# A first cluster assignment of two heads on split partitions, another order of the first loads, and other planner costs, in a kernel of clustered attention and two MLPs

## The chip, the cores and the metric

The kernel runs on one core of a Trainium2 chip. The metric is the device time of one execution in microseconds. Engines: TensorE (PE in the rows, its weight loads PEld), VectorE (DVE), ScalarE (ACT), GpSimd (POOL) and SyncE (SP), which here issues every DMA, one after the other on one queue.

## The reference, cut to what matters

Attention has 2 batches, 8 heads, 768 positions and 64 columns a head. Every query and key is put into one of 16 clusters of its head, and a query sees only the keys of its own cluster. The output (1536 tokens by 512) goes through a squared-ReLU MLP (512 to 2048 to 512) and a gated MLP (512 to 1536 to 512).

```python
q_assign = np.argmax(np.einsum('bhsd,hcd->bhsc', q_n, c_n), axis=-1)
k_assign = np.argmax(np.einsum('bhsd,hcd->bhsc', k_n, c_n), axis=-1)
mask = q_assign[:, :, :, None] == k_assign[:, :, None, :]
scores = np.where(mask, scale * np.matmul(q, k.transpose(0, 1, 3, 2)), -1000000000.0)
attn = np.exp(scores - np.max(scores, axis=-1, keepdims=True))
attn = attn / (np.sum(attn, axis=-1, keepdims=True) + 1e-09)
x = np.matmul(attn, v)              # then laid out as tokens x 512
h = np.maximum(x @ w_in, 0.0)
x = h * h @ w_out
out = (1.0 / (1.0 + np.exp(-(x @ w_gate))) * (x @ w_val)) @ w_out2
```

## The kernel before

**Tiles.** A score tile is 128 queries by 768 keys of one head: 96 tiles, numbered 0 to 95, six a head (n // 6 is the head, batch 0 first). For each, TensorE makes `s` (`t_qk`, L821), VectorE the negative row maximum `nm` (`t_max`), ScalarE the exponential (`t_exp`), ScalarE an upper f16 part `hl` (`t_hi`) and VectorE the lower f16 part into the same `hl` (`t_lo`). A DMA transpose turns two tiles into `pt` (`t_turn`, L878), TensorE multiplies them by the values into `po` (`t_pv`), and VectorE scales `po` into `xp` (`t_x`). The pairs of tiles in the list `by_pe` take another way: TensorE transposes the f32 tile (`tb`, L906), and nothing is split.

**The mask** is part of the score product. A head has query rows `T` and key rows `M`: 64 rows of numbers, split into a rounded part and a remainder by subtraction (`qlo` L776, `klo` L782), and 16 rows that say which cluster a column belongs to. Copies on ScalarE, VectorE or GpSimd build these tiles for head 1 and later heads (the helper `copy` has L317, L319 and L321 for the three engines); DMAs put the cluster rows in (`dup`, L752, L753). Head 0 has its own tile `TM`.

**The assignment** of four heads is one group. TensorE writes 16 dots a column into `as` (`assign_dots`, L419): 128 partitions are 2 (queries or keys) x 2 pairs of heads x 32, and the 768 columns lie in two halves of 384. VectorE then does seven steps over 128x768 (`assign_steps`, L440: transpose `d`, maximum `mx`, `eq`, `w`, maximum `m`, `eq`, transpose back `ot`), after which two writes at 16x768 fill `TM` (L559 and the copy behind it) and `assign_end` (L498) makes `oh` for the other heads. Group 0 is written out by hand before the planner starts and needs the loads of two pairs of heads.

**Magnitudes of the values.** ScalarE takes |v| of the six tiles of a batch (`v_abs`, L510, tile `jk`); VectorE reduces them to `a` (L515), TensorE and VectorE make a scale `sc` of it, by which the values are split in two f16 parts `vh`, `vl`.

**Weights** come as 64-bit words in staging tiles (two of them during attention, tiles `wi0r`, `wo0r`), are turned to f32 (L1172 to L1201), and split in two parts (`wi0h`, `wi0l`). The first MLP runs on chunks of 512 tokens. Chunk 0 (batch 0's first tokens) is worked into the attention of batch 1: `g` is a block of the first product, `y` of the second. `xq` are the transposes of the attention's output. From the fourth `y` group of chunk 0 on (`y0_3`) only MLP work is left, and TensorE does it in a fixed order.

**The order** of all that follows group 0 is made when the program is built. `Planner` keeps a list of tasks, each with a cost in ns for every engine that could do it (`{"v": 869, "p": 1660}`) and a priority (tile number minus an offset from `PLAN`); it starts on each engine the ready task with the lowest priority and adds `SETTLE` until a result can be read. A task may only move to another engine if it would end sooner there by its price (cost plus offsets). Tasks of VectorE and GpSimd that use a shared port are not planned side by side (`port`). `Planner({...})` (L253) holds the planned time at which each engine is free after the part by hand. On the chip every engine then runs its list in order and waits for semaphores.

## Time and profile before

| | us |
|---|---|
| median of 3 runs (830.93 to 834.58) | 832.7 |
| profiled execution | 831.97 |
| its span, first to last instruction | 830.2 |
| TensorE busy | 766.0 (92%) |
| VectorE busy | 547.9 (66%) |
| ScalarE busy | 447.8 (54%) |
| GpSimd busy | 266.4 (32%) |

The profiled execution is 1.8 us longer than its span. Busy shares are means over two stages that differ: attention with chunk 0 of the MLP worked in, up to about 345 us, and the rest of the MLPs. The mean granted clock of TensorE is 0.968 of 2.4 GHz over the span.

### The profile page before, as it was taken

What the parts mean: (1) busy time and instruction counts of PE and PEld (TensorE: products, weight loads), DVE (VectorE), ACT (ScalarE), POOL (GpSimd) and SP (SyncE); (2) the same over time, 40 slices, a digit from 0 to 9 for tenths busy, and PEclk for the clock granted to TensorE, in tenths of its full rate; (3) what the DMA queues carried; (4) which work ended last, traced back from release to release, by engine and by line L of the source; (5) the groups of instructions that cost most, each with busy time, mean ns of one, the idle gap of its engine ahead of it and who ended that gap; (6) DMA issues with size and microseconds to landing.
All of it is one profiled execution on the core that took longest, in us unless ns stands there. A gap on an engine that the chain in (4) does not pass through costs nothing.

```text
span 830.2 us, 12473 instructions
## 1 busy us (share of the span) xinstructions
PE 766.0 (92%) x4721; PEld 633.7 (76%) x4721; DVE 547.9 (66%) x865; ACT 447.8 (54%) x800; POOL 266.4 (32%) x322
## 2 busy tenths in 40 slices
PE   8778687789888979799999999999999999999998
PEld 4468576668776868688888888888888888888886
DVE  5689888989999998868376776924333427933300
ACT  2989767778887675758564563422212225612300
POOL 3955646486555323334041322111111113100000
PEclk9889789999999989999999999999999999999999
DMA  6599997966889788732232322411211222100101
GB/s 201 137 191 211 181 191 158 214 130 137 165 207 212 180 194 185 268 102 95 83 127 76 102 80 98 135 68 54 98 51 51 76 78 102 51 24 27 39 26 38
DMA packets 143420, 100.56 MB, mean 121 GB/s; under 512 B 124128, under 2 KB 124128, under 8 KB 143360
## 3 DMA queue, kind: packets, MB, share of 16 engines
q1 hardware_dynamic: 143360, 99.76, 47.4%
q8 instruction: 37, 0.61, 0.3%
q14 instruction: 23, 0.19, 0.1%
HBM read 62.10 MB, written 3.15 MB: 79 GB/s over the span
## 4 chain that ended last, share of the span: by engine, by line
PE 68%; DVE 11%; DMA 8%; ACT 6%; issue 4%; POOL 1%; SPq 1%; DVEq 0%; POOLq 0%; ACTq 0%
PE y L310 14%; PE o L310 12%; PE pv L310 12%; PE pg L310 12%; PE g L310 11%; DMA pt<-hl 5%; DVE nm L839 3%; PE po L310 3%; PE s L310 3%; DMA wo0r<-in_moe_w_out_dram 2%; DVE hl L869 2%; ACT s L854 2%; ACT hl L317 2%; DMA raw<-in_k_dram 1%; DVE M L319 1%
## 5 line engine op out<-in xcount | busy, mean ns | idle before, releaser
L310 PE MATMUL s<-M,T 128*128 128x384 f32 x360 | 88.5, 375 | 28.2 <-DVE hl L869 14.2
L839 DVE TENSOR_REDUCE nm<-s 128x1 f32<-128x768 f32 x96 | 90.3, 950 | 10.6 <-PE s L310 9.9
L310 PEld LDWEIGHTS s<-M,T 128*128 128x128 f32 x360 | 65.2, 204 | 38.8 <-issue 14.1
L1442 DVE SCALAR_TENSOR_TENSOR gv<-th,pv 128x512 f32<-128x512 f32 x36 | 24.6, 687 | 98.2 <-PE pv L310 98.2
L1435 ACT ACTIVATE th<-pg 128x512 f32<-128x512 f32 x36 | 21.5, 598 | 123.9 <-PE pg L310 120.1
L854 ACT ACTIVATE s<-s,nm 128x768 f32<-128x768 f32 x78 | 68.1, 873 | 24.1 <-DVE nm L839 23.7
L869 DVE TENSOR_TENSOR hl<-s,hl 128x768 f16<-128x768 f32 x78 | 73.7, 948 | 4.0 <-ACT hl L317 3.6
L310 PEld LDWEIGHTS <-pt 128*128 128x128 f16 x1404 | 49.4, 104 | 24.0 <-DMA pt<-hl 13.8
L310 PE MATMUL po<-vh,pt 128*128 128x64 f16 x936 | 53.9, 202 | 13.8 <-DMA pt<-hl 9.1
L317 ACT ACTIVATE hl<-s 128x768 f16<-128x768 f32 x78 | 63.3, 811 | 1.9
L310 PE MATMUL po<-vl,pt 128*128 128x64 f16 x468 | 51.0, 202 | 0.0
L1471 ACT ACTIVATE ot<-o 128x512 f32<-128x512 f32 x12 | 7.2, 599 | 81.0 <-PE o L310 81.0
L1369 ACT ACTIVATE r<-g 128x512 f32<-128x512 f32 x48 | 28.7, 598 | 26.5 <-PE g L310 26.4
L1180 POOL TENSOR_SCALAR wgm<-wgm 128x512 f32<-128x512 f32 x12 | 7.7, 643 | 104.5 <-ACT wgm L1172 92.9
L1411 DVE TENSOR_TENSOR yf<-yf,y 128x512 f32<-128x512 f32 x36 | 24.7, 685 | 17.9 <-PE y L310 17.5
L776 POOL TENSOR_TENSOR T<-raw,T 64x768 fp32r<-64x768 f32 x15 | 29.3, 1954 | 4.1 <-ACT T L317 3.1
L782 POOL TENSOR_TENSOR M<-raw,M 64x768 fp32r<-64x768 f32 x15 | 28.3, 1887 | 1.4 <-DVE M L319 0.5
L1375 ACT ACTIVATE g<-r 128x512 f32<-128x512 f32 x47 | 28.3, 601 | 0.9
L1298 DVE TENSOR_TENSOR gs_0l<-gv,gs_0h 128x512 fp32r<-128x512 f32 x3 | 2.1, 690 | 39.3 <-ACT gs_0h L317 39.3
L1180 POOL TENSOR_SCALAR wi1m<-wi1m 128x512 f32<-128x512 f32 x16 | 10.4, 652 | 52.6 <-ACT wi1m L1172 45.6
L310 PEld LDWEIGHTS po<-vr,ptf 128*128 128x128 f32 x216 | 25.6, 192 | 0.2 <-DVE xp L961 0.2
L310 PE MATMUL po<-vr,ptf 128*128 128x64 f32 x216 | 25.6, 272 | 0.0
(583 smaller groups left out, 2359.5 us busy)
## 6 DMA issues: line engine op xcount, KB each, us to landing
wi0r<-in_moe_w_in_dram SPq DMA_DIRECT2D x16, 512.0 KB, 4.3
wo0r<-in_moe_w_out_dram SPq DMA_DIRECT2D x16, 512.0 KB, 4.0
wi1r<-in_moe_w_in_dram SPq DMA_DIRECT2D x16, 512.0 KB, 3.4
wo1r<-in_moe_w_out_dram SPq DMA_DIRECT2D x16, 512.0 KB, 3.3
wgr<-in_moe_w_gate_dram SPq DMA_DIRECT2D x12, 512.0 KB, 3.2
wvr<-in_moe_w_val_dram SPq DMA_DIRECT2D x12, 512.0 KB, 4.2
w2r<-in_moe_w_out_dram SPq DMA_DIRECT2D x12, 512.0 KB, 4.0
raw<-in_q_dram SPq DMA_DIRECT2D x8, 384.0 KB, 4.0
```

The source lines that it names most:

```text
L310: nc.tensor.matmul(o, lhsT=l, rhs=r, start=a, stop=z)
L317: nc.scalar.activation(out=out, in_=in_, func=AF.Copy, scale=scale)
L776: eng(e).tensor_tensor(out=T1[j][q], in0=raw[k][r], in1=T1[j][r].bitcast(F32), op=ALU.subtract)
L782: eng(e).tensor_tensor(out=M2[j][r], in0=raw[k][r], in1=M1[j][r].bitcast(F32), op=ALU.subtract)
L839: nc.vector.tensor_reduce(out=NM[n], in_=sc_ps[n][:, :, :HS], axis=AX.XY, op=ALU.max, negate=True)
L854: nc.scalar.activation(out=y, in_=x, func=AF.Exp, bias=NM[n], accum_out=SM[n // NQ][:, i : i + 1],)
L869: nc.vector.tensor_tensor(out=halves(hl[:, n % 2, 1]), in0=x[:, :, :HS], in1=halves(hl[:, n % 2, 0]), op=ALU.subtract,)
L1369: nc.scalar.activation(out=r, in_=banks["g1", c, f], func=AF.Relu)
L1375: nc.scalar.activation(out=p, in_=r, func=AF.Square)
L1411: nc.vector.tensor_tensor(out=yf[c, dm], in0=yf[c, dm], in1=p, op=ALU.add)
L1435: nc.scalar.activation(out=t, in_=p, func=AF.Tanh, scale=0.5)
L1442: nc.vector.scalar_tensor_tensor(out=o, in0=t, scalar=1.0, in1=p, op0=ALU.add, op1=ALU.mult)
```

## The change

The first group is cut in two. `pair_dots` makes the dots of two heads only, and puts the two halves of the 768 columns on different partitions, so that the seven steps run over 128x384. Heads 2 and 3 become a group of their own (numbered -1 in the code; its tiles are called `d4`, `ot4`, `oh4` in the built program), which the planner places. `oh` of these two groups is half as wide; its rows go to a head by four DMAs instead of two. The by-hand `oh` of the first group moves to GpSimd.

The first loads are issued in another order: queries and keys of the first pair of heads, the keys of head 0 for `TM`, the six value tiles, and then the second and third pair. Before, the second pair stood ahead of the values. A table load for the exponential is asked for early by a one-column activation (`warm`). The products that keep TensorE busy during the first assignment are 7 instead of 11 and read the keys instead of the queries.

The planner gets other costs (loads, DMA transposes, subtractions on GpSimd), other offsets in `PLAN` (nearly all of some 70; one line of them is shown), other times of the first tasks, a list `by_pe` of ten pairs instead of nine, and a reserve of slabs for the first chunk (`xn`). `NS`, `e_bufs` and `third` come to the same numbers as before, and `by_pool` is empty.

```diff
-SETTLE = {"t": 200, "v": 120, "a": 130, "p": 130, "q": 2500}
+SETTLE = {"t": 200, "v": 120, "a": 130, "p": 130, "q": 2100}
...
+    "asg_p": -800, "assign": 15, "assign_step": 2.0, "base": 70, "build": 4, "build2": 5.9,
...
-    "by_pe": (1, 7, 8, 16, 19, 24, 26, 30, 33,),
+    "by_pe": (1, 7, 10, 13, 16, 19, 24, 26, 30, 33,),
...
-    NS = 34
+    NS = 37 - (3 * PLAN["e_bufs"] + 1) // 2
...
-    WARM = (10, 11)
+    WARM = (10, 7)
...
-    plan = Planner({"t": 16300, "v": 16700, "a": 5600, "p": 6500, "q": 14100})
+    plan = Planner({"t": 13900, "v": 14000, "a": 5600, "p": 13600, "q": 17500})
...
+    units.update({"xn": 2 * KD})
...
-    for p in range(2):
-        for s in range(2):
-            load_raw(s, 0, p)
+    for s in range(2):
+        load_raw(s, 0, 0)
     nc.sync.dma_start(out=MN[0:64], in_=kT[0, 0, 0:64])
     for t in range(NQ):
         load_v(0, t)
-    for s in range(2):
-        load_raw(s, 0, 2)
+    for p in range(1, 3):
+        for s in range(2):
+            load_raw(s, 0, p)
...
+    warm = at.tile([P, 1], F32, name="warm")
+    nc.scalar.activation(out=warm, in_=rt, func=AF.Exp, scale=0.0)
...
+    def pair_dots(gp):
+        a = s_tile(f"as_{-gp}")
+        for s in range(2):
+            for hf in range(2):
+                r0 = s * 64 + hf * 32
+                mm(
+                    a[r0 : r0 + 32, 0, :HS], CB[:, -gp].rearrange("p j c -> p (j c)"),
+                    raw[s, 0, -gp][:, hf * HS : (hf + 1) * HS], True, True,
+                )
+        assign_tiles(gp, a)
...
-        OH[gp] = at.tile([P, S], F32, tag="oh", name=f"oh{gp}")
+        n = S if gp > 0 else HS
+        OH[gp] = at.tile([P, S], F32, tag="oh", name=f"oh{gp % (NG + 1)}")
         eng(e).tensor_scalar(
-            out=OH[gp], in0=AS[gp]["ot"], scalar1=aux_a, scalar2=aux_b, op0=ALU.mult, op1=ALU.add
+            out=OH[gp][:, :n], in0=AS[gp]["ot"][:, :n], scalar1=aux_a, scalar2=aux_b,
+            op0=ALU.mult, op1=ALU.add,
...
-    assign_dots(0)
+    pair_dots(0)
     nc.scalar.activation(out=TN[0:64], in_=raw[0, 0, 0][0:64], func=AF.Copy, scale=0.125)
-    keep_busy(raw[0, 0, 0][:, :HS], WARM[1])
+    keep_busy(raw[1, 0, 0][:, :HS], WARM[1])
     drop(busy)
-    for f, _ in assign_steps(0, 1):
+    for f, _ in assign_steps(0, 2):
         f(0)
     drop(AS[0]["a"])
     ot = AS[0]["ot"]
-    nc.vector.tensor_scalar(
-        out=MN[64 : 64 + C], in0=ot[64 : 64 + C], scalar1=BIG, scalar2=-BIG,
-        op0=ALU.mult, op1=ALU.add,
-    )
-    copy("v", TN[64 : 64 + C], ot[0:C])
-    assign_end(0)
+    for hf in range(2):
+        c = slice(hf * HS, (hf + 1) * HS)
+        nc.vector.tensor_scalar(
+            out=MN[64 : 64 + C, c], in0=ot[64 + 32 * hf : 64 + 32 * hf + C, :HS],
+            scalar1=BIG, scalar2=-BIG, op0=ALU.mult, op1=ALU.add,
+        )
+        copy("v", TN[64 : 64 + C, c], ot[32 * hf : 32 * hf + C, :HS])
+    assign_end(0, "p")
...
-                    lambda e, s=s, b=b, p=p: load_raw(s, b, p), {"q": 1092},
+                    lambda e, s=s, b=b, p=p: load_raw(s, b, p), {"q": 1600},
...
-    ohhold = {0: hold("oh", 1, 3)}
-    for gp in range(1, NG):
-        b, gr = divmod(gp, H // 4)
+    ohhold = {0: hold("oh", 1, 1)}
+    for gp in [-1] + list(range(1, NG)):
+        b, gr = divmod(max(gp, 0), H // 4)
         keys = [(s, b, 2 * gr + pl) for s in range(2) for pl in range(2)]
         pr = 24 * gp - PLAN["assign"]
+        if gp < 0:
+            keys = [(s, 0, 1) for s in range(2)]
+            pr = 12 - PLAN["assign"]
+        parts = 1 if gp > 0 else 2
...
-            cost = (930, 869, 869, 469, 869, 869, 869)[k]
+            cost = (930, 869, 869, 869, 869, 869, 869)[k] // parts + 65 * (parts - 1)
...
-        gp = hd // 4
+        gp = hd // 4 if hd > 3 else -(hd // 2)
...
+            if gp <= 0:
+                for t, o1 in ((T2[j], j * C), (M2[j], 64 + j * C)):
+                    for hf in range(2):
+                        nc.sync.dma_start(
+                            out=t[a, hf * HS : (hf + 1) * HS].bitcast(F32),
+                            in_=OH[gp][o1 + 32 * hf : o1 + 32 * hf + C, :HS],
+                        )
+                return
...
-                qlo, {"v": 869, "p": 1660}, kind="qk_lo", prio=pr + PLAN["build2"], after=[t0],
+                qlo, {"v": 869, "p": 1880}, kind="qk_lo", prio=pr + PLAN["build2"], after=[t0],
...
-                dup, {"q": 900}, pr, after=[t0] + ([assigned[gp]] if gp else []),
+                dup, {"q": 1400 if gp > 0 else 2000}, pr, after=[t0] + ([assigned[gp]] if gp else []),
...
-                lambda e, p=p: t_turn(e, p), {"q": 3500}, n - PLAN["turn"], after=[prev_lo, lo],
+                lambda e, p=p: t_turn(e, p), {"q": 4300}, n - PLAN["turn"], after=[prev_lo, lo],
...
-                lambda e: self.load(f), {"q": 1456}, pr - PLAN["w_load"], take=[("st", 1)],
+                lambda e: self.load(f), {"q": 2100}, pr - PLAN["w_load"], take=[("st", 1)],
```

What stands on VectorE's list at the end of the first assignment, before (`TM` is head 0's tile, `a1` the reduced magnitudes, `nm0` the first row maximum, `M1` the keys of a later head):

```order
L559 TENSOR_SCALAR TM_1_113<-ot0_221 16x768
L319 TENSOR_SCALAR TM_1_113<-ot0_221 16x768
L498 TENSOR_SCALAR oh0_246<-ot0_221,aux_a_170,aux_b_171 128x768
L515 TENSOR_REDUCE a10_284<-am0_255 128x1
L319 TENSOR_SCALAR M1_0_109<-M1_0_109 64x768
L839 TENSOR_REDUCE nm0_39_294<-s0_36_281 128x1
L839 TENSOR_REDUCE nm1_44_304<-s1_38_291 128x1
```

and now:

```order
L590 TENSOR_SCALAR TM_1_113<-ot0_219 16x384
L329 TENSOR_SCALAR TM_1_113<-ot0_219 16x384
L544 TENSOR_REDUCE a10_268<-am0_246 128x1
L885 TENSOR_REDUCE nm0_35_270<-s0_33_262 128x1
L828 TENSOR_TENSOR M2_1_112<-raw1_0_0_3_118,M1_1_110 64x768
L554 TENSOR_REDUCE a30_281<-pa0_39_276 1x1
L555 TENSOR_SCALAR a30_281<-a30_281 1x1
```

The writes of `TM` are four of half the width (the last two are shown), `oh` is gone from this list, the copy `M1` too, and the first maximum stands right behind the reduction of the magnitudes; a subtraction for `M2` of head 1 has come in.

On ScalarE's list, from head 0's queries to the first value tiles (`jk`), before:

```order
L552 ACTIVATE TM_1_113<-raw0_0_0_2_116 64x768
L317 ACTIVATE raw0_0_0_2_116<-raw0_0_0_2_116 128x768
L317 ACTIVATE T1_1_106<-raw0_0_0_2_116 64x768
L317 ACTIVATE M1_1_110<-raw1_0_0_3_118 64x768
L317 ACTIVATE T1_0_105<-raw0_0_1_4_120 64x768
L510 ACTIVATE jk0_0_21_256,am0_255<-vr0_0_6_125 128x512
L510 ACTIVATE jk0_1_23_258,am0_255<-vr0_1_7_127 128x512
```

and now:

```order
L581 ACTIVATE TM_1_113<-raw0_0_0_2_116 64x768
L327 ACTIVATE raw0_0_0_2_116<-raw0_0_0_2_116 128x768
L327 ACTIVATE T1_1_106<-raw0_0_0_2_116 64x768
L327 ACTIVATE M1_1_110<-raw1_0_0_3_118 64x768
L539 ACTIVATE jk0_0_20_247,am0_246<-vr0_0_4_121 128x512
L327 ACTIVATE T2_1_108<-T1_1_106 64x768
L539 ACTIVATE jk0_1_22_250,am0_246<-vr0_1_5_123 128x512
L539 ACTIVATE jk0_2_24_252,am0_246<-vr0_2_6_125 128x512
```

The copies for the second pair of heads (`T1_0` from `raw0_0_1`) are behind the values, and a copy `T2_1` has come from GpSimd.

On SyncE's list at the end of the attention, from one load of `w_in` to the last of `w_out` for chunk 0, before:

```order
L1162 DMA wi0r14_1257_4118<-in_moe_w_in_dram 128x512
L878 DMA_TRANSPOSE pt46_1266_4145<-hl92_1237_4069 128x24x128
L1162 DMA wi0r15_1279_4208<-in_moe_w_in_dram 128x512
L1162 DMA wo0r12_1303_4238<-in_moe_w_out_dram 128x512
L878 DMA_TRANSPOSE pt47_1313_4287<-hl94_1265_4143 128x24x128
L1162 DMA wo0r13_1323_4330<-in_moe_w_out_dram 128x512
L1162 DMA wo0r14_1331_4349<-in_moe_w_out_dram 128x512
L1162 DMA wo0r15_1338_4363<-in_moe_w_out_dram 128x512
```

and now:

```order
L934 DMA_TRANSPOSE pt46_1269_4166<-hl92_1252_4091 128x24x128
L1228 DMA wi0r14_1285_4209<-in_moe_w_in_dram 128x512
L934 DMA_TRANSPOSE pt47_1289_4221<-hl94_1279_4193 128x24x128
L1228 DMA wi0r15_1318_4306<-in_moe_w_in_dram 128x512
L1228 DMA wo0r12_1323_4318<-in_moe_w_out_dram 128x512
L1228 DMA wo0r13_1331_4366<-in_moe_w_out_dram 128x512
L1228 DMA wo0r14_1337_4387<-in_moe_w_out_dram 128x512
L1228 DMA wo0r15_1348_4410<-in_moe_w_out_dram 128x512
```

The loads `wi0r15` and `wo0r12` stood ahead of the last DMA transpose, `pt47`, and now stand behind it.

Over the stage up to the last lower part of chunk 0's `g` (`g0_15l`), the two lists of VectorE differ by kind as follows (counted on the built programs; rows that are equal are left out, and the steps of the assignment, whose total width is the same):

| on VectorE | before | after |
|---|---|---|
| subtractions for `T` and `M`, 64x768 | 0 | 9 |
| copies `M<-raw`, 64x768 | 8 | 2 |
| copies `T<-raw`, 64x768 | 5 | 0 |
| copies `M<-M`, 64x768 | 2 | 4 |
| `vh`, 128x256 | 6 | 2 |
| lower parts `hl`, 128x768 | 78 | 76 |
| lower parts of weights `wi0l`, `wo0l`, 128x512 | 15 | 21 |

GpSimd has 21 subtractions for `T` and `M` instead of 30. On TensorE the sequence of blocks from `xq1_0` to the end is the same in both programs, and 336 products of the MLP stand ahead of it in both; ahead of score tile 95 stand 264 before and 240 now.

## Rows read from the trace of the kernel before

**Rows 1.** Stretches: their length, then each engine's busy us, clock, DMA share, GB/s

```profile
0.00:345.00 345.00, 285.18 (x2606) 235.81 (x2607) 300.34 (x465) 258.19 (x470) 182.45 (x225) 0.93 0.84 186
345.00:830.20 485.20, 480.85 (x2117) 397.88 (x2115) 247.53 (x401) 189.57 (x332) 83.91 (x97) 1.00 0.22 75
```

**Rows 2.** VectorE's timeline at the start: start us, us, line, operation [idle before]

```profile
10.85 1.05 DVE L455 STREAM_TRANSPOSE d<-as 128x384 f32<-128x384 f32 x2 [4.14 <-PE as L310]
...
16.56 0.98 DVE L488 STREAM_TRANSPOSE ot<-eq 128x768 f16<-128x768 f16 x1
17.65 0.55 DVE L559 TENSOR_SCALAR TM<-ot 16x768 f32<-16x768 f16 x1
...
25.23 0.16 DVE L515 TENSOR_REDUCE a<-am 128x1 f32<-128x6 f32 x1 [5.75 <-ACT jk L510]
...
26.93 0.96 DVE L839 TENSOR_REDUCE nm<-s 128x1 f32<-128x768 f32 x1
```

**Rows 3.** Timeline of TensorE at the start, same columns

```profile
6.77 1.74 PE L310 MATMUL as<-raw,CB 128*32 128x384 f32 x12 [0.55 <-DVE CB L413]
9.34 1.48 PE L310 MATMUL as<-raw,CB 128*32 128x384 f32 x4 [0.83 <-DMA raw<-in_k_dram]
10.74 7.36 PE L310 MATMUL busy<-raw,ident 128*128 128x384 f32 x22
19.02 1.53 PE L310 MATMUL s<-TM 128*128 128x384 f32 x4 [0.92 <-DVE TM L319]
```

**Rows 4.** Timeline of ScalarE at the start, same columns

```profile
18.21 0.84 ACT L317 ACTIVATE raw<-raw 128x768 f32<-128x768 f32 x1 [12.98 <-PE busy L310]
...
21.43 0.61 ACT L510 ACTIVATE jk<-vr 128x512 f32<-128x512 f32 x1
...
26.68 1.28 ACT L854 ACT_TABLE_LOAD   x1
```

**Rows 5.** The first 15 us in stretches of 5

```profile
0.00:5.00 5.00, 3.63 (x17) 3.63 (x18) 2.11 (x15) 2.10 (x3) 4.28 (x27) 1.00 0.56 177
5.00:10.00 5.00, 3.62 (x20) 1.73 (x20) 0.98 (x3) 0.23 (x1) 2.04 (x3) 1.00 0.99 277
10.00:15.00 5.00, 5.00 (x16) 2.69 (x15) 3.93 (x6) 0.00 (x0) 0.00 (x0) 1.00 0.99 373
```

**Rows 6.** Groups on VectorE: xcount, busy us, mean ns, idle before

```profile
L869 DVE TENSOR_TENSOR hl<-s,hl 128x768 f16<-128x768 f32 x78 | 73.7, 948 | 4.0 <-ACT hl L317 3.6
...
L319 DVE TENSOR_SCALAR M<-raw 64x768 fp32r<-64x768 f32 x8 | 7.8, 972 | 0.2
...
L1245 DVE TENSOR_TENSOR wo0l<-wo0m,wo0h 128x512 fp32r<-128x512 f32 x10 | 7.2, 720 | 0.1
...
L319 DVE TENSOR_SCALAR M<-M 64x768 fp32r<-64x768 f32 x2 | 3.0, 1516 | 0.6 <-ACT M L317 0.6
...
L319 DVE TENSOR_SCALAR T<-raw 64x768 fp32r<-64x768 f32 x5 | 2.8, 559 | 0.1
L319 DVE TENSOR_SCALAR vh<-vr,sc 128x256 f16<-128x256 f32 x6 | 2.5, 439 | 0.0
```

**Rows 7.** The same for GpSimd's subtractions

```profile
L776 POOL TENSOR_TENSOR T<-raw,T 64x768 fp32r<-64x768 f32 x15 | 29.3, 1954 | 4.1 <-ACT T L317 3.1
```

**Rows 8.** The same for TensorE's transposes of the pairs in by_pe

```profile
L906 PE MATMUL tb<-ident,e 128*128 128x128 f32 x108 | 17.6, 286 | 4.4 <-ACT e L854 1.8 <-ACT ptf L317 1.8 <-DVE a L525 0.7
```

**Rows 9.** VectorE's waits from 26.9 to 344 us: total, times, longest

```profile
DVE nm L839 <- PE s L310: 9.9, 11, 2.5
```

**Rows 10.** End of the attention stage, VectorE

```profile
321.14 0.96 DVE L839 TENSOR_REDUCE nm<-s 128x1 f32<-128x768 f32 x1
```

**Rows 11.** The same stretch, SyncE's queue

```profile
325.02 4.45 SPq L878 DMA_TRANSPOSE pt<-hl  x1
329.56 1.48 SPq L1162 DMA_DIRECT2D wo0r<-in_moe_w_out_dram  x3
```

**Rows 12.** The chain of waits, 340 to 350 us: start, length, what

```profile
345.99 3.58 PE y L310 x12
```

More of the change, by code (lines that the diff above doesn't have):

```diff
@@ L581 @@
             for s in range(2):
-                first = b == 0 and p == 0
-                k = 3 if first else 5
-                if b == 0 and p < 2:
-                    k -= 1
+                k = 2 if b == 0 and p == 0 else 5
                 rawhold[s, b, p] = hold("raw", 1, k)
@@ L621, with step @@
         t = add(
-            dots, {"t": 2200}, pr, after=[x for k in keys for x in raw_after(*k)],
-            take=[("s", 1), ("asg", 1)], give=[rawhold[k] for k in keys],
+            dots, {"t": 2200 // parts}, pr, after=[x for k in keys for x in raw_after(*k)],
+            take=[("s", 1), ("asg", 1)], give=[rawhold[k] for k in keys], at=max(raw_at(*k) for k in keys),
         )
         for k in range(7):
-            def step(e, gp=gp, k=k):
-                f = assign_steps(gp, 1)[k][0]
+            def step(e, gp=gp, k=k, parts=parts):
+                f = assign_steps(gp, parts)[k][0]
                 f(0, e) if k == 3 else f(0)
@@ L645 @@
     by_pe = [p for p in range(NT // 2) if BYPE(p)]
+    by_pool = [n for n in PLAN["by_pool"] if n // 2 not in by_pe]
     pe_pairs = [sum(p * 2 // (H * NQ) == b for p in by_pe) for b in range(B)]
@@ L788 @@
             scaled[kq] = add(
-                lambda e, k=kq: copy(e, raw[k], raw[k], 0.125), {"a": 790, "p": 850}, pr - 0.5,
-                kind="qk_sc", after=raw_after(*kq),
+                lambda e, k=kq: copy(e, raw[k], raw[k], 0.125), {"a": 790, "p": 900}, pr - 0.5,
+                kind="qk_sc", after=raw_after(*kq), at=raw_at(*kq),
             )
         t0 = add(
-            qhi, {"a": 790, "v": 469, "p": 850}, pr, kind="qk_hi", after=[scaled[kq]], take=[(f"T{j}", 1)],
+            qhi, {"a": 790, "v": 469, "p": 900}, pr, kind="qk_hi", after=[scaled[kq]], take=[(f"T{j}", 1)],
             give=[rawhold[kq]],
@@ L863, in t_hi @@
             HL[n // 2] = tile_of("hl", (P, 2, 2, S), F16, f"hl{n}")
-        copy(e, halves(HL[n // 2][:, n % 2, 0]), sc_ps[n][:, :, :HS])
+        if n in by_pool:
+            copy(e, HL[n // 2][:, n % 2, 0], ET[n])
+        else:
+            copy(e, halves(HL[n // 2][:, n % 2, 0]), sc_ps[n][:, :, :HS])
     def t_lo(e, n):
         hl = HL[n // 2]
+        if n in by_pool:
+            x = ET.pop(n)
+            eng(e).tensor_tensor(
+                out=hl[:, n % 2, 1], in0=x, in1=hl[:, n % 2, 0], op=ALU.subtract
+            )
+            drop(x)
+            return
         x = sc_ps.pop(n)
@@ L1065 @@
         dd = add(
-            lambda e, hd=hd: t_d(e, hd), {"p": 200}, hd * NQ + PLAN["d"], after=et, take=[("d", 1)], give=[smh]
+            lambda e, hd=hd: t_d(e, hd), {"p": 350 + 350 * sum((hd * NQ // 2 + x in by_pe) != (hd * NQ // 2 + x + 1 in by_pe) for x in range(NQ // 2 - 1))}, hd * NQ + PLAN["d"], after=et, take=[("d", 1)], give=[smh]
         )
@@ L1140, in near, with spare @@
         return lambda: k <= pos[0] + ahead
+    def spare(k, n):
+        return k <= pos[0] + 1 and units["xn"] == 0 or units["S"] >= n + SPARE + units["xn"]
     def pr_of(k, early):
@@ L1215, in room @@
             def room():
[L1216 removed]
+                return k <= pos[0] + CONVGATE and spare(k, 1)
             t = add(
@@ L1251, in split_tasks @@
             a = add(
-                hi, {"a": 520, "v": 335, "p": 610}, pr_of(k, PLAN["w_split"]), after=[self.conv[f]], take=[("S", 1)], kind="w_hi",
-                give=mh, gate=near(k, SPLITGATE),
+                hi, {"a": 520, "v": 335, "p": 700}, pr_of(k, PLAN["w_split"]), after=[self.conv[f]], take=[("S", 2)], kind="w_hi",
+                give=mh, gate=lambda: k <= pos[0] + SPLITGATE and spare(k, 2),
             )
             b = add(
-                lo, {"v": 602, "p": 1270}, pr_of(k, PLAN["w_split"]), after=[a], take=[("S", 1)], give=mh, kind="w_lo",
+                lo, {"v": 602, "p": 1370}, pr_of(k, PLAN["w_split"]), after=[a], give=mh, kind="w_lo",
             )
@@ L1262, in done, with split_bank @@
                 drop(t)
-    def split_bank(table, key, p, label, pr, after, give):
+    def split_bank(table, key, p, label, pr, after, give, take=()):
         def hi(e):
```

114 lines of the change are left out of this document (66 added, 48 removed).

## The prediction

> **What bounds the kernel now.** I read the page's shares and slices first, then the stretches, the start's timeline, and VectorE's groups and waits. The stretches part the program in two [rows 1]: to 345 us TensorE is idle for 59.8 us; behind that it is busy for 480.85 of 485.2 us at full granted clock. The second part is TensorE's own work in an order that the change leaves alone, so it stays as it is. The end moves by as much as `y0_3` does, which now starts at 345.99 us [rows 12]; the rest of the span, 484.2 us, follows it.
>
> To 345 us VectorE is the fullest engine, 300.34 us busy [rows 1]. Its 44.7 idle us lie in two places. Before its first row maximum at 26.93 us it waits 4.14 us for the dots and 5.75 us for the last magnitude [rows 2], beside the time until the first load. What is left, some 30 us after that maximum, is in small pieces; the largest sum is 9.9 us for scores [rows 9]. So I price the change in VectorE's time: when it starts on the score tiles, how much work it has from there, and how much it waits.
>
> **The start, before.** The dots come in two lots, since the fourth load lands late: 1.74 us of 12 products at 6.77, 1.48 of 4 at 9.34 [rows 3]. The seven steps run from 10.85 to 17.54 [rows 2]. ScalarE meanwhile stands: its copy of the queries waits until 18.21 for the products that keep TensorE busy and read them [rows 4, 3]. Three copies later it takes the magnitudes from 21.43, each 0.61 us [rows 4]. Their reduction stands in VectorE's list ahead of the first maximum, so VectorE is idle until 25.23.
>
> **The start, now.** Only the first two loads are needed, and they were there at 6.77. Half the products, half of 1.74 + 1.48, are 1.6 us (0.9 if only the dense lot counts): the dots end at 8.4. The steps at half width are half of 6.7 us with some launch time on top, 3.5, and the four writes of `TM` at half of 0.55 us [rows 2] and a little more each are 1.1: `TM` is ready near 13.0. The busy products, 7/11 of 7.36 us [rows 3], end near 13.1, and the first scores take 1.53: 14.6. That is not the last to arrive. ScalarE is free at 8.4, as the busy products now read the keys. It does five copies of 0.84 and six magnitudes of 0.61 and some read-out: 8.4 + 4.2 + 3.7 + 0.2 = 16.5. The first maximum follows the reduction (0.16) at about 16.9, where it was at 26.93: **10 us earlier**. The values must have landed: what is asked for up to the last value tile is 0.03 + 2 x 0.39 + 0.20 + 6 x 0.26 = 2.6 MB; the queue moved 0.9 MB in the first 5 us and 1.4 in the next [rows 5], and 0.3 more at 373 GB/s takes 0.9: 10.9 us, while the sixth magnitude needs its tile at 15.7. The second pair's loads, 0.8 MB behind, land near 13. The early table load costs 1.28 us in the shade of VectorE's work on the centroids; it takes 1.28 off ScalarE's path at 26.68 [rows 4], which is in these 10 us only if ScalarE is late there, so I count it at nothing. Bounds of the whole term: 8 (if dots and copies take their longer forms) to 11.
>
> **VectorE's work after the first maximum**, up to the last lower part of `g`:
> - nine subtractions come from GpSimd. VectorE has none in this trace. The nearest are `hl` with the same 768 columns, 948 ns, and `wo0l` with 512 columns and both inputs in SBUF, 720 ns, which would be 1.08 us at 768 [rows 6]; far off is GpSimd's own 1954 [rows 7]. I take 0.95: +8.6; bounds +8.6 and +17.6.
> - eleven copies go: 6 x 0.972 + 5 x 0.559 = -8.6 [rows 6].
> - three more `M<-M` fall behind the first maximum (four where one was there), at about 1 us: the mean is 1.516, but of two, and `T<-raw` of that size takes 0.559 [rows 6]: +3 (1.7 to 4.5).
> - four `vh` less, -1.8; two `hl` less, -1.9; six more lower parts of weights, 6 x 0.72 = +4.3 [rows 6].
> - the second group's steps, about 3 us, were before the first maximum and now are behind it: +3.
>
> The sum is 8.6 - 8.6 + 3 - 1.8 - 1.9 + 4.3 + 3 = **+6.6 us**, so most of the early start is filled with work.
>
> The Trainium skill ("SBUF — State Buffer", section "Who interferes with whom") speaks against the first item: a VectorE instruction with two inputs in SBUF and a GpSimd instruction that reads SBUF shut each other out, the second waiting for the whole of the first. The trace agrees so far as copies of one size take 559 and 972 ns [rows 6]; for subtractions only a rival below says what it would cost.
>
> **VectorE's waits after the first maximum.** They are about 30 us. Loads and transposes are now planned longer, so less should be started too early; GpSimd has nine subtractions of 1.95 us less [rows 7] beside VectorE. Against that, ScalarE takes eleven more copies of 0.84 [rows 4], some 9 us in a stage where it is busy 258.19 of 345 [rows 1]. I take -3, with bounds of -9 and +4.
>
> One more pair goes by TensorE: its twelve transposes are 17.6/9 = 2.0 us [rows 8], under the 59.8 idle us; without that cover they cost 2.0. Fewer DMAs copy `M`, four small ones replace two: nothing, while SyncE's queue waits for VectorE more than VectorE for it. The reserve `xn` and the load costs for later weights act behind 345 us, where TensorE hardly waits.
>
> **Sum:** -10 + 6.6 - 3 = -6.4. The span of 830.2 becomes 823.8; 1.8 us lie around it, 825.6 for the profiled execution; the median of the runs is 0.7 above it (832.7 against 831.97): **826.3**.
>
> **Rivals.**
> - *The gain is given back at the tail.* Now 24.85 us pass from the last maximum, 321.14 [rows 10], to `y0_3` [rows 12]: exponential, split, a transpose that holds SyncE's queue for 4.45 us, then three loads at 329.56 [rows 11], whose conversion ends the stage. Now five loads stand behind that transpose, and 24 products fewer are done by then. Two further tiles are to be converted there, each by five to six VectorE instructions of about 0.7 [rows 6], some 8 us. If nothing before makes it up (no fewer waits): the work of VectorE is the same sum, but the extra lies on a chain of loads that VectorE cannot fill; -10 + 8 = -2: 830.7. For it speaks the order; against, that VectorE's lists up to the last maximum weigh the same, so that this maximum may come over 10 us earlier.
> - *The second group comes late.* Heads 2 and 3 now need GpSimd's `oh4` and four DMAs behind two transposes of about 4.45 us each [rows 11]. No row tells when they land. Every us that they are late is one of the end's, as VectorE has only score tiles to do there; one transpose too late costs 4.45: 830.8. Against it: the planner places this group far ahead of its use, with the longer DMA costs.
> - *Waits fall more.* At -9 instead of -3: 820.3. The planner's corrected costs speak for it; ScalarE's added copies against.
> - *Slower: the moved subtractions are held by GpSimd.* At 1.95 us each, GpSimd's own time [rows 7], nine of them cost 17.6 instead of 8.6, and the waits stay: -10 + 15.6 = +5.6: 838.3. It is slower than before from a mean of about 1.33 us a subtraction (0.95 + 3.4/9). The skill's rule would do that if nearly each met a GpSimd instruction. Against it: lower parts of weights with two SBUF inputs take 720 ns at 512 columns, close to what `hl` gives per column [rows 6].
>
> **How the numbers follow.** Forecast (823 to 829) 0.46, waits fall more 0.17, given back at the tail 0.17, second group late 0.10, slower 0.10. Half a per cent, 4.2 us, is what a measurement can tell here. Faster by that (below 828.5): nearly all of the forecast and the second case, 0.61; within it the tail, the late group and half of the last, 0.32; slower 0.07. The range from 819.0 to 833.5 leaves out the ends of the second case and the last one.
>
> **What would show it.** Right: the first maximum near 17 us, magnitudes done near 16.5, subtractions on VectorE near 0.95 us, `y0_3` near 340, and 484 us from there to the end. Wrong: a first maximum after 20 us; a mean of the subtractions above 1.3; VectorE idle ahead of tile 12's maximum; more than 27 us from the last maximum to `y0_3`; TensorE idle for more than 2 us between `y0_3` and the last product.

## Result and the profile after

| | before | after |
|---|---|---|
| median of the runs (lowest to highest) | 832.86 us (830.93 to 834.58, 4 runs) | 823.08 us (820.98 to 826.14, 4 runs) |
| profiled execution, span | 831.97, 830.2 | 824.81, 823.0 |
| first row maximum | 26.93 | 16.37 |
| first product of `y0_3` | 345.99 | 338.73 |
| from there to the end of the span | 484.2 | 484.3 |

The ratio is 0.989, 95% interval 0.986 to 0.992. A second series, together with other kernels, gave 825.83 us (824.48 to 828.46, 6 runs) and 0.994 (0.992 to 0.996). So the change makes the kernel faster, by 1.1% in the one series and 0.6% in the other; forecast were 826.3 us, 0.8%. The profiled executions differ by 7.2 us, the medians of the two series by 9.8 and 5.2.

The two stretches, parted at 339 us, 0.3 us behind the start of `y0_3` (before at 345, 1.0 ahead of it; columns as in [rows 1]):

```profile
0.00:339.00 339.00, 283.92 (x2603) 237.77 (x2604) 303.19 (x474) 269.80 (x495) 164.65 (x220) 0.92 0.83 183
339.00:823.00 484.00, 479.99 (x2112) 397.19 (x2110) 246.81 (x404) 188.69 (x330) 75.26 (x89) 1.00 0.22 74
```

The second stretch is the old one. The first ends 7.3 us earlier by the start of `y0_3`, although VectorE is 2.9 us and ScalarE 11.6 us busier in it; GpSimd has lost 17.8 us. VectorE's start, beside [rows 2]:

```profile
8.00 0.58 DVE L482 STREAM_TRANSPOSE d<-as 128x384 f32<-128x384 f32 x1 [1.28 <-PE as L320]
...
11.45 0.58 DVE L515 STREAM_TRANSPOSE ot<-eq 128x384 f16<-128x384 f16 x1
12.13 0.35 DVE L590 TENSOR_SCALAR TM<-ot 16x384 f32<-16x384 f16 x1
...
12.88 0.55 DVE L590 TENSOR_SCALAR TM<-ot 16x384 f32<-16x384 f16 x1
13.46 1.87 DVE L329 TENSOR_SCALAR TM<-ot 16x384 f32<-16x384 f16 x1
16.29 0.16 DVE L544 TENSOR_REDUCE a<-am 128x1 f32<-128x6 f32 x1 [0.97 <-ACT jk L539]
16.37 0.95 DVE L885 TENSOR_REDUCE nm<-s 128x1 f32<-128x768 f32 x1
```

(The first two rows are the first and the last of the seven steps.) The steps begin at 8.00 instead of 10.85 and take 4.0 us instead of 6.7; the wait for the magnitudes has shrunk from 5.75 to 0.97. ScalarE's first copy starts at 8.00 instead of 18.21 [rows 4], and nothing but the first maximum stands ahead of the first exponential:

```profile
8.00 0.84 ACT L327 ACTIVATE raw<-raw 128x768 f32<-128x768 f32 x1 [2.41 <-PE as L320]
...
16.07 0.19 ACT L539 ACTIVATION_READ_ACCUMULATOR jk<-vr 128x1 f32 x1
17.35 0.88 ACT L900 ACTIVATE s<-s,nm 128x768 f32<-128x768 f32 x1 [1.09 <-DVE nm L885]
```

The end of the stage in the chain of waits, beside [rows 12]:

```profile
336.10 0.61 DVE g_15l L1342
336.71 0.04 issue
336.76 1.97 PE xq L1152 x8
338.73 6.30 PE y L320 x21
```

**One sum for all kernels below.** VectorE works in list order, so its last lower part, `g_15l`, starts at: first maximum + VectorE's busy time from there + its waits from there. In 12 of the 14 profiles here 486 to 487 us of the span follow it. In g3 it is 494, as VectorE there still has twelve instructions on the weights `wo0` behind `g_15l`, so that the mark comes before the end of the stage; in f2, with 490, it has three, and none to two in the others. I read each kernel by these three terms; a window of the trace from the first maximum to `g_15l` gives the busy time (third busy figure), and length less busy time is the wait:

```profile
16.37:336.03 319.66, 268.17 (x2542) 226.95 (x2542) 291.10 (x442) 256.21 (x469) 153.36 (x187) 0.92 0.83 179
```

Here: 16.37 + 291.10 + 28.56 = 336.03. Of before: 26.93 + 286.33 + 30.11 = 343.37. So the start gave -10.56, the work took +4.77, the waits gave -1.55, together -7.34.

| kernel | first maximum | work | waits | `g_15l` | median, us (runs) | ratio to before |
|---|---|---|---|---|---|---|
| before | 26.9 | 286.3 | 30.1 | 343.4 | 832.86 (4) | 1 |
| changed | 16.4 | 291.1 | 28.6 | 336.0 | 823.08 (4) | 0.989 (0.986 to 0.992) |
| the same again, g1 | 16.5 | 293.1 | 30.1 | 339.6 | 825.83 (6) | 0.994 (0.992 to 0.996) |
| the start alone, e1 | 15.6 | 285.5 | 41.6 | 342.7 | 832.27 (10) | 1.001 (0.999 to 1.004) |
| the rest alone, e2 | 22.1 | 290.7 | 48.6 | 361.4 | 849.17 (4) | 1.020 (1.017 to 1.023) |
| changed, VectorE held, e3 | 29.1 | 291.2 | 27.7 | 348.0 | 840.25 (4) | 1.010 (1.006 to 1.015) |
| changed, queries read, g2 | 23.2 | 290.8 | 30.8 | 344.8 | 835.92 (10) | 1.005 (1.003 to 1.008) |
| before, keys read, f3 | 25.5 | 281.7 | 32.7 | 339.9 | 830.49 (10) | 0.999 (0.996 to 1.001) |
| changed, subtractions on GpSimd, e4 | 16.2 | 286.8 | 39.5 | 342.5 | 831.12 (10) | 0.997 (0.994 to 1.000) |
| changed, loads on another queue, f4 | 15.8 | 290.9 | 31.0 | 337.6 | 829.92 (10) | 0.996 (0.993 to 0.999) |
| changed, planned 880, f1 | 15.8 | 289.9 | 34.8 | 340.5 | 824.95 (4) | 0.989 (0.982 to 0.996) |
| changed, planned 850, g3 | 15.4 | 288.3 | 37.5 | 341.2 | 836.85 (7) | 1.007 (1.005 to 1.010) |
| before, planned 880, f2 | 27.8 | 280.8 | 38.6 | 347.1 | 838.24 (10) | 1.009 (1.006 to 1.011) |
| before, planned 850, g4 | 27.7 | 283.4 | 32.0 | 343.2 | 828.58 (10) | 0.998 (0.996 to 1.001) |

Start, work, waits and `g_15l` are of one profiled execution each, which may lie some us off the median; the ratios are to runs of the kernel before on the same chip. Work and waits scatter too: VectorE's list of the kernel before is also that of f3, with 4.6 us less work, and the list of the changed kernel was profiled five times (changed, g1, e3, g2, f4), with 290.8 to 293.1 us of work and 27.7 to 31.0 us of waits.

### The profile page after: what moved, and what is told of

It reads as the page before. It is cut to its first block, busy times and chain, and to the rows that moved or that the text cites. A ratio compares the mean times of both kernels' runs of the same rounds, so it can differ in the third digit from the quotient of the medians.

```text
span 823.0 us, 12416 instructions
## 1 busy us (share of the span) xinstructions
PE 763.9 (93%) x4713; PEld 635.0 (77%) x4713; DVE 550.0 (67%) x877; ACT 458.5 (56%) x824; POOL 239.9 (29%) x309
## 4 chain that ended last, share of the span: by engine, by line
PE 59%; DVE 0%; ACT 0%; issue 0%
PE y L320 12%; PE pv L320 12%; PE o L320 12%; PE pg L320 12%; PE g L320 11%; PE xq L1152 0%; DVE g_15l L1342 0%; ACT ot L1538 0%
## 5 line engine op out<-in xcount | busy, mean ns | idle before, releaser
L925 DVE TENSOR_TENSOR hl<-s,hl 128x768 f16<-128x768 f32 x76 | 72.0, 950 | 5.5 <-ACT hl L327 5.2
L320 PEld LDWEIGHTS <-pt 128*128 128x128 f16 x1368 | 47.6, 103 | 18.7 <-issue 9.4
L327 ACT ACTIVATE hl<-s 128x768 f16<-128x768 f32 x76 | 60.9, 814 | 1.0
L320 PE MATMUL po<-vh,pt 128*128 128x64 f16 x912 | 51.5, 201 | 9.7 <-DMA pt<-hl 7.7
L320 PE MATMUL po<-vl,pt 128*128 128x64 f16 x456 | 48.8, 201 | 0.0
L1436 ACT ACTIVATE r<-g 128x512 f32<-128x512 f32 x48 | 28.7, 597 | 30.1 <-PE g L320 30.0
L320 PE MATMUL po<-vr,ptf 128*128 128x64 f32 x240 | 31.6, 287 | 2.5 <-ACT ptf L327 1.3
L320 PEld LDWEIGHTS po<-vr,ptf 128*128 128x128 f32 x240 | 31.3, 206 | 3.0 <-DVE xp L1017 1.6
L1311 POOL TENSOR_TENSOR wvl<-wvm,wvh 128x512 fp32r<-128x512 f32 x10 | 12.9, 1290 | 50.3 <-ACT wvh L327 43.3
L962 PE MATMUL tb<-ident,e 128*128 128x128 f32 x120 | 20.2, 290 | 5.7 <-ACT ptf L327 4.2
L822 POOL TENSOR_TENSOR T<-raw,T 64x768 fp32r<-64x768 f32 x11 | 20.8, 1888 | 5.5 <-ACT T L327 4.1
```

The lines of the kernel that those rows point to most:

```text
L320: nc.tensor.matmul(o, lhsT=l, rhs=r, start=a, stop=z)
L327: nc.scalar.activation(out=out, in_=in_, func=AF.Copy, scale=scale)
L822: eng(e).tensor_tensor(out=T1[j][q], in0=raw[k][r], in1=T1[j][r].bitcast(F32), op=ALU.subtract)
L925: nc.vector.tensor_tensor(out=halves(hl[:, n % 2, 1]), in0=x[:, :, :HS], in1=halves(hl[:, n % 2, 0]), op=ALU.subtract,)
L962: nc.tensor.transpose(t[:, x * P : (x + 1) * P], ET[2 * p + u][:, kt * P : (kt + 1) * P], ident)
L1436: nc.scalar.activation(out=r, in_=banks["g1", c, f], func=AF.Relu)
```

## Experiments

### The two halves of the change, each alone

The start alone (e1) is the kernel before with `pair_dots`, the load order, the busy products on the keys and the early table load, but with the old `PLAN`, costs and pairs:

```diff
+    pair_dots(0)
+    keep_busy(raw[1, 0, 0][:, :HS], WARM[1])
+    for gp in [-1] + list(range(1, NG)):
 ...
     "by_pe": (1, 7, 8, 16, 19, 24, 26, 30, 33,),
```

> The kernel before with the new start alone: two heads assigned first on split partitions, the loads in order of use, the busy products on the keys, the early table load, and the second group of heads 2 and 3 behind it. The planner's numbers, its costs and the nine pairs stay as they were, so its order is made anew from an earlier start; VectorE gets no subtractions of T and M. Theory A (the end follows VectorE: its start, its work and its waits up to the last lower part of g): first maximum near 16.4 us, 10.5 earlier, less 3 us for the second group's steps that now lie behind it, with a scatter of some 3 us for the order made anew: about 825.5 us, 822 to 829. Theory B (the tail's chain of transposes and loads sets the end, and the gain came from the planner's numbers): the early start is lost again in the tail, 831 to 834.

The rest alone (e2) is its counterpart: new `PLAN` (45 of its 81 offsets have new values and four were added, fewer than "nearly all"), new costs, ten pairs, and the old start.

```diff
-    "by_pe": (1, 7, 8, 16, 19, 24, 26, 30, 33,),
+    "by_pe": (1, 7, 10, 13, 16, 19, 24, 26, 30, 33,),
+SETTLE = {"t": 200, "v": 120, "a": 130, "p": 130, "q": 2100}
 ...
     assign_dots(0)
     keep_busy(raw[0, 0, 0][:, :HS], WARM[1])
```

> The kernel before with everything but the new start: the planner's new numbers, the longer DMA and GpSimd costs, ten pairs by TensorE; first assignment of four heads, load order, busy products and table load as before. Theory A: the first maximum stays near 26.9 us; VectorE's added work and the shorter waits nearly cancel (about +2 and -2 us), so about 833 us, 829 to 837. Theory B: most of the gain of 9.8 us is here: 823 to 827.

Measured: 832.27 us for the start alone, 849.17 us for the rest alone, and 823.08 for both. Theory A missed both, theory B the second. The windows from first maximum to `g_15l`, first of e1:

```profile
15.60:342.71 327.11, 266.26 (x2542) 223.83 (x2542) 285.49 (x429) 252.50 (x458) 175.48 (x201) 0.93 0.84 183
```

and of e2:

```profile
22.13:361.41 339.28, 280.51 (x2538) 237.21 (x2536) 290.69 (x445) 258.83 (x478) 155.35 (x184) 0.88 0.76 168
```

The work came as the sum has it, and in e1 the start too: e1 starts 11.3 us earlier and works 0.8 us less, e2 works 4.4 us more, like the changed kernel, and has the nine subtractions on VectorE, of which e1 has none. In e2 the first maximum came at 22.1 us and not, as expected, at 26.9: in its order it stands ahead of the reduction of the magnitudes, and the wait for these falls behind it:

```profile
26.77 0.16 DVE L525 TENSOR_REDUCE a<-am 128x1 f32<-128x6 f32 x1 [3.69 <-ACT jk L520]
```

What missed are the waits: 41.6 us in e1 and 48.6 in e2 (3.7 of them that wait) where 30.1 and 28.6 were. VectorE's longest waits of e1:

```profile
DVE nm L873 <- PE s L310: 14.9, 22, 4.4
DVE xp L995 <- PE po L310: 11.2, 11, 5.1
DVE hl L903 <- ACT hl L317: 7.0, 12, 1.6
```

and of the changed kernel, from the first maximum on:

```profile
DVE nm L885 <- PE s L320: 10.2, 16, 1.5
DVE xp L1017 <- PE po L320: 5.5, 8, 2.7
DVE hl L925 <- ACT hl L327: 5.2, 14, 0.9
```

Scores, products with the values and ScalarE's halves: each kind is longer in e1, none is one place. So the whole early start went into small waits. In e2 TensorE is also slower: 280.5 us busy for 2538 products at a granted clock of 0.88, where the changed kernel needs 268.2 for 2542 at 0.92. Whether the low clock made the waits there or followed from them these runs don't tell; the last section comes back to it.

### Does the end follow the first maximum when the order is kept?

Three kernels shift the first maximum and keep the order of all other instructions. e3 adds work without use to VectorE ahead of it:

```diff
+    for _ in range(24):
+        nc.vector.tensor_reduce(
+            out=AS[0]["mx"][:, : HS // C, 0],
+            in_=AS[0]["d"][:, :HS].rearrange("p (g c) -> p g c", c=C), axis=AX.X, op=ALU.max,
+        )
     units["S"] -= NQ
```

> The changed kernel, its order of instructions as it is, with 24 row maxima of 384 columns put into VectorE's list ahead of the first score's maximum (work without use, some 10 us). This holds VectorE alone; the other engines start as early as in the changed kernel. Theory A: what VectorE loses at the start it loses at the end, nearly us for us: the first maximum comes some 9 to 11 us later and the run takes 830 to 834 us. Theory B: the tail's chain has slack for it: 823 to 827.

Timeline of VectorE:

```profile
15.05 14.06 DVE L597 TENSOR_REDUCE mx<-d 128x24 f32<-128x384 f32 x24
29.04 0.15 DVE L544 TENSOR_REDUCE a<-am 128x1 f32<-128x6 f32 x1
29.10 0.95 DVE L890 TENSOR_REDUCE nm<-s 128x1 f32<-128x768 f32 x1
```

The first maximum comes 12.73 us later (the 24 took 14.06, not 10), `g_15l` 11.94 later, the span 12.3. The waits are 27.7 us, 0.9 less. The median, 840.25 of four runs from 837 to 845, lies 17 above the changed kernel's first series and 14 above its second, and so above theory A's 830 to 834. Four us of that are the longer hold; the rest isn't explained, but the runs were granted a lower clock, 0.949 to 0.961 over the span against 0.967 to 0.979 and 0.962 to 0.969 of the changed kernel's two series. By the profile theory A holds, and theory B is out.

g2 puts back what the busy products read:

```diff
-    WARM = (10, 7)
+    WARM = (10, 11)
-    keep_busy(raw[1, 0, 0][:, :HS], WARM[1])
+    keep_busy(raw[0, 0, 0][:, :HS], WARM[1])
```

> The changed kernel, its order as it is, with the 11 products that keep TensorE busy reading the queries again, as in the kernel before. ScalarE's first copy then waits until about 15.4 us instead of 8.0 and the magnitudes end near 23.7. Theory A (what the first maximum loses, the end loses): first maximum near 24 us, 7.5 later, and 829 to 832 us. Rival G (GpSimd, whose work starts from ScalarE's copies, starts later too and no longer holds VectorE's writes of the first operands, and the waits that follow shrink): 824 to 827 us.

ScalarE's first copy waited:

```profile
14.89 0.84 ACT L327 ACTIVATE raw<-raw 128x768 f32<-128x768 f32 x1 [9.36 <-PE busy L320]
```

The first maximum is at 23.24, 6.9 us later, `g_15l` 8.7 later than in the first profile of the changed kernel and 5.1 later than in the second; the median is 10.1 us above the 825.83 beside it. Theory A again, 4 us above its range. Rival G is out: GpSimd no longer holds the last write of `TM` there (0.35 us instead of 1.87), but the waits are 30.8 us, not fewer. So about 7 of the start's 10.6 us hang on what these products read and how many they are; the other 3.7 (two heads, narrower steps, order of loads) were not taken apart.

f3 makes the same edit, the other way, in the kernel before (7 products, on the keys):

> The kernel before, its order of instructions as it is, with one part of the new start alone: the products that keep TensorE busy read the keys and are 7 instead of 11, so that ScalarE's copy of the queries no longer waits for them. Magnitudes then end near 18 us, the first maximum comes near 20.7 us, some 6 us earlier. Theory A: VectorE's list moves as a whole: 826 to 828 us. Theory D in its strong form (the order's waits take back what the start gains, since the loads and transposes behind it do not move): VectorE's waits after the first maximum grow by 4 to 6 us and the time stays at 831 to 834 us.

The first maximum came only 1.4 us earlier, not 6. ScalarE did start at 8.26, and GpSimd's copies and subtractions run from 10.13 on instead of 20.08, so that they now lie beside VectorE's steps and its writes of `TM`. VectorE, beside the 0.55 us each in [rows 2]:

```profile
18.42 1.84 DVE L559 TENSOR_SCALAR TM<-ot 16x768 f32<-16x768 f16 x1
20.27 2.06 DVE L319 TENSOR_SCALAR TM<-ot 16x768 f32<-16x768 f16 x1
```

and GpSimd:

```profile
18.05 1.79 POOL L776 TENSOR_TENSOR T<-raw,T 64x768 fp32r<-64x768 f32 x1
19.92 1.99 POOL L782 TENSOR_TENSOR M<-raw,M 64x768 fp32r<-64x768 f32 x1
```

Each write ends 0.42 us after the GpSimd instruction that was there before it. With two steps that took 0.98 and 1.46 us instead of 0.56 and 0.96, `TM` is ready 3.6 us later than before. Another 1.4 us come from TensorE: with fewer busy products and a later `TM` it is idle for 7.2 us ahead of the first scores, and these four products take 2.90 us at a granted clock of 0.50, where they took 1.53 at 1.00 [rows 3]:

```profile
22.58 2.90 PE L310 MATMUL s<-TM 128*128 128x384 f32 x4 [7.22 <-DVE TM L319]
...
22.50:25.50 3.00, 2.92 (x6) 1.53 (x7) 1.16 (x3) 0.00 (x0) 0.00 (x0) 0.50 0.17 33
```

Neither theory was tested as meant; the median, 830.49, can't be told from before. In the changed kernel the same hold is there once, in the write of 1.87 us at 13.46, and costs nothing, since the magnitudes end later still.

### The nine subtractions

e4 keeps the order of the changed kernel and issues them on GpSimd:

```diff
-            eng(e).tensor_tensor(
+            nc.gpsimd.tensor_tensor(
                 out=T1[j][q], in0=raw[k][r], in1=T1[j][r].bitcast(F32), op=ALU.subtract
```

(and the same for `M2`).

> The changed kernel, its order as it is, but the nine subtractions of T and M that went to VectorE are issued on GpSimd again. VectorE has 9.9 us less to do (nine at a mean of 1.10). Theory A in its plain form: each us off VectorE counts, and the run takes 813 to 818 us. Rival C: these subtractions are due at once, on GpSimd (1.95 us each, behind what it has) the heads' operands come later, and VectorE waits for scores instead of working: 822 to 832 us, with more than 10 us of VectorE's waits for products of the scores added.

831.12 us, in rival C's range; theory A in its plain form is out. VectorE's groups of the changed kernel first:

```profile
L828 DVE TENSOR_TENSOR M<-raw,M 64x768 fp32r<-64x768 f32 x5 | 5.8, 1170 | 0.1
...
L822 DVE TENSOR_TENSOR T<-raw,T 64x768 fp32r<-64x768 f32 x4 | 4.1, 1023 | 0.1
...
L329 DVE TENSOR_SCALAR M<-M 64x768 fp32r<-64x768 f32 x4 | 3.1, 774 | 0.1
...
L329 DVE TENSOR_SCALAR M<-raw 64x768 fp32r<-64x768 f32 x2 | 1.1, 554 | 0.0
```

then of e4, and the largest sum of its waits (total, times, longest):

```profile
L329 DVE TENSOR_SCALAR M<-M 64x768 fp32r<-64x768 f32 x4 | 5.1, 1264 | 1.1 <-ACT M L327 1.0
...
L329 DVE TENSOR_SCALAR M<-raw 64x768 fp32r<-64x768 f32 x2 | 2.0, 987 | 0.0
...
DVE nm L885 <- PE s L320: 13.9, 21, 1.6
```

9.9 us went from VectorE, but its copies beside the longer GpSimd list grew by 2.8, and in all its work fell by only 4.3; the remainder is small groups and the overlap of neighbouring instructions. Its waits grew by 10.9 us. Rival C put more than 10 us of that on the scores; these waits grew by 3.7, those for products with the values by 4.2 (to 9.7) and those for ScalarE's halves by 2.3 (to 7.5), so its reason is shown in part only. Taking these subtractions over was worth 6.5 us by `g_15l` (342.53 against 336.03) in this order, and 2.9 against the second profile of the changed kernel.

### The tail

f4 takes the five loads of weights behind the last transpose off SyncE's queue:

```diff
-            nc.sync.dma_start(out=t, in_=src)
+            q = nc.scalar if late and self.name in ("wi0", "wo0") else nc.sync
+            q.dma_start(out=t, in_=src)
```

> The changed kernel, its order as it is, with the five loads of weights that SyncE issues behind the last transpose put on ScalarE's DMA queue. Theory T (the tail is bound by these loads behind the transpose): from the last maximum to y0_3 some 30 us instead of 33.4, VectorE's waits there 1 us instead of 4.3, and the run about 820 us. Theory V (VectorE's work of converting five tiles fills the tail, so the loads' start hardly matters): 822 to 824 us.

SyncE's queue of the changed kernel, beside [rows 11]:

```profile
310.90 3.65 SPq L934 DMA_TRANSPOSE pt<-hl  x1
314.64 0.53 SPq L1228 DMA_DIRECT2D wi0r<-in_moe_w_in_dram  x1
315.22 2.94 SPq L1228 DMA_DIRECT2D wo0r<-in_moe_w_out_dram  x4
```

In f4, where ScalarE issues them in its own order (its queue):

```profile
311.48 0.39 ACTq L1233 DMA_DIRECT2D wi0r<-in_moe_w_in_dram  x1
...
317.15 0.35 ACTq L1233 DMA_DIRECT2D wo0r<-in_moe_w_out_dram  x1
...
325.69 0.33 ACTq L1233 DMA_DIRECT2D wo0r<-in_moe_w_out_dram  x1
```

One load leaves 3.2 us earlier, the others 2 to 8 us later, and the stretch is 1.8 us longer (305.18 to 337.64 against 305.37 to 336.03, 6.2 us of waits instead of 4.3). By its profile theory V, since VectorE works 26.4 us in this stretch in the one and 26.3 in the other; the median, 829.92 with runs from 825 to 835, is worse than V expected. That loads which are early for all five would bring nothing isn't shown.

### Other orders from the same numbers

The planner makes its order from planned costs, so I moved one of them, a row maximum's, in both kernels:

```diff
-            mx = add(lambda e, n=n: t_max(e, n), {"v": 865}, ...
+            mx = add(lambda e, n=n: t_max(e, n), {"v": 880}, ...
```

(850 in g3 and g4).

> The changed kernel with one number of its planner moved: the planned cost of a score tile's row maximum 880 ns instead of 865. The work is the same; the order made from it differs from about tile 17 on. Theory D (an order's waits depend on how its numbers were fitted to each other, and an order made anew from slightly other numbers waits some 10 us more, whatever the start): first maximum near 16.4 us, VectorE's work up to the last lower part of g within 3 us of 291, its waits at 35 to 45 instead of 28.6 us; 829 to 840 us. Theory A (the new start and the new costs are worth their us in any order): 821 to 827 us.

> The kernel before with the same one number moved (880 ns instead of 865). Theory D: first maximum near 26.9 us, work near 286, VectorE's waits at 40 or more instead of 30.1 us, so about 842 us, 836 to 852; the kernel with the new start alone (832.3), whose order is as unfitted, is then some 10 us faster than this one, which is what the start is worth. Theory A: 830 to 835 us.

> The changed kernel with the planned cost of a row maximum at 850 ns instead of 865, a third order from the same numbers (it differs from tile 6 on). Theory D' (an order made anew costs the changed kernel 0 to 4 us): waits of 28 to 36 us, 822 to 829 us. Theory D (10 us): 830 us or more.

> The kernel before with the planned cost of a row maximum at 850 ns instead of 865, a third order from its numbers. If its own order is a fitted one, as the 838.2 us at 880 say: 836 to 842 us, waits of 36 to 42; the new start alone, in an order made anew as well (832.3), is then worth about 6 us. If 838.2 was one bad order: 830 to 834 us.

> The changed kernel once more, as it is, beside the next kernels on one chip, to see how its executions scatter: 821 to 827 us, a ratio to the kernel before of 0.986 to 0.993.

Measured: the changed kernel 823 and 826 in its own order (the second just above the ratio expected), 825 at 880 and 837 at 850; the kernel before 831 to 833 in its own, 838 at 880 and 829 at 850. The waits go from 28.6 to 37.5 and from 30.1 to 38.6; g3 loses 6.7 us more behind `g_15l`. The orders also move work between engines: in f2 VectorE has 5.6 us less of it, and in f1 five subtractions instead of nine, so that waits and work trade places in these kernels. Theory D was right on f2 by its time (its waits, 38.6, fall short of 40) and, against D', on g3, and wrong on f1 by its median, though the profiled one of f1's runs (819 to 829 us), the longest, waits 34.8 us. g4 came out below even the "one bad order" answer to f2, 830 to 834. So beside runs on the same chip an order made anew moved the time by +11 (g3), +6 (f2) and -2 us (g4); f1 had no run of the changed kernel beside it, and its ratio to the kernel before, 0.989, is that of the first series. The edit moves one planned cost by 15 ns, and the 5 to 10 us of the change lie within what it did. e1 and e2 were such orders too: that the start alone shows no gain says that this order waits 11.5 us more, not that the start is worth nothing.

## Why the prediction was right, and where its steps were off

- **The second stretch and the tie to `y0_3`.** As forecast: 484.3 us follow it, and TensorE is busy without a break for 480.26 us, from 338.73 to the end of its last product at 818.99.
- **The start, -10.** Measured -10.56. Magnitudes were done at 16.26 (16.5 forecast), the reduction followed at 16.29. What the first score tile needs of `TM` was there at 13.43 (13.0 forecast), and its products began at 13.10 with the first half of the keys. The last write, the second half of the queries, ended at 15.33: the hold by GpSimd was not in the sum, and VectorE had only 1 us of idle time left to cover it.
- **VectorE's work, +6.6.** Measured +4.8 between the two profiles, from the same terms with other sizes (against f3's profile of the old list it would be +9.4). Subtractions 9.9 (8.6): the mean is 1.10, not 0.95. Copies -9.5 (-8.6). `M<-M` +1.0 (+3): the one behind the first maximum of before took 2.10 us beside a GpSimd subtraction; of the four now one does so, with 1.41 us, and the others take 0.55 to 0.58. `vh` and `hl` -3.1 (-3.7). Lower parts of weights +6.0 (+4.3), as their mean rose from 0.709 to 0.794. The second group's steps 3.5 (3). Not priced at all: an `oh` of another group, +0.7, and the 64 instructions that put together the weights' words, which became shorter, 0.758 to 0.715 on average, -2.8. The rest, -1.1, is small groups and the overlap of neighbouring instructions. The terms were off by 0.5 to 2.8 us, and most of their errors cancelled.
- **The waits, -3.** Measured -1.55, inside the bounds. This is the term on which the result hung, and the prediction's reasons for it ("loads and transposes are now planned longer") don't carry it: the same costs with the old start gave +18.5, or +14.8 without the wait for the magnitudes. The bounds of -9 to +4 were too narrow for what an order can do: e1 and e2 lie beyond them, and even f1 and g3, the changed kernel itself, at +4.7 and +7.4.
- **Given back at the tail (0.17).** Its mechanism is there: from the last maximum, 305.37, to `y0_3` it takes 33.36 us instead of 24.85, 8.5 us more, as the rival had it. But the last maximum came 15.8 us earlier, for the reason given against the rival: work only went from ahead of it to behind it, where VectorE is busy for 26.4 us up to `g_15l` instead of 18.7. The sign "more than 27 us from the last maximum to `y0_3`" was a wrong one; such a stretch says nothing without what was moved into it.
- **Second group late (0.10).** It wasn't. The small transfers of heads 2 and 3 start in SyncE's queue so:

```profile
42.99 1.17 SPq L793 DMA_DIRECT2D T<-oh  x2
44.21 1.21 SPq L793 DMA_DIRECT2D M<-oh  x2
```

and VectorE comes to tile 12's maximum without a wait:

```profile
49.64 0.95 DVE L885 TENSOR_REDUCE nm<-s 128x1 f32<-128x768 f32 x1
```

- **Slower, subtractions held (0.10).** The mean, 1.10, lies between 0.95 and the 1.33 from which this rival decides. Five of the nine took 0.95. Four took 1.23 to 1.35: they were issued while GpSimd was working, and each ended 0.80 to 0.81 us after the GpSimd instruction that was there before it. (One of the five began 0.10 us before the end of one, and took 0.95.) One of each, VectorE:

```profile
119.05 1.31 DVE L828 TENSOR_TENSOR M<-raw,M 64x768 fp32r<-64x768 f32 x1
...
146.34 0.95 DVE L828 TENSOR_TENSOR M<-raw,M 64x768 fp32r<-64x768 f32 x1
```

and GpSimd beside the first, which ends at 119.56, 0.80 us before it:

```profile
118.73 0.83 POOL L331 TENSOR_SCALAR M<-M 64x768 fp32r<-64x768 f32 x1 [1.70 <-ACT M L327]
```

The Trainium skill ("SBUF — State Buffer", section "Who interferes with whom") says of two inputs in SBUF that whoever issues second is blocked until the first is done. The four long ones agree with it (the copies of 559 and 972 ns, which the prediction read as agreement, have one input, and so are another case); as each waited for the rest of a short GpSimd instruction and not for a whole long one, the price was 0.28 to 0.40 us.
- **Waits fall more (0.17).** They didn't: -1.55 and not -9.

So the prediction was right in the start and in its tie to the end, right in the work by errors that cancelled, and right in the waits by a number for which it had no good reason.

## What to carry to other kernels

With the order kept, the end followed the first instruction of the bounding engine nearly us for us (in e3, 12.7 late gave 12 late; in g2, 6.9 late gave 5 to 9). A build that makes its order anew draws new waits, here 28 to 49 us for nearly the same work, so price the start and the work by rows, give the waits a range as wide as the orders show, and test a change of order against other orders before crediting its idea. An edit that lets one engine start earlier also starts the others earlier: look at what the third engine will then do beside the bounding one, and whether TensorE falls idle.
